# Retention and a SwiGLU feed-forward on one core: an inner level of seven products for three of six gate/value groups in the last two units

## The chip, the cores and the metric

The kernel runs on one core of a Trainium2 chip. The metric is device time in microseconds: the median over several executions. All data are float32. The engines are named as in the profile: PE (TensorE matmuls), PEld (TensorE weight loads), DVE (VectorE), ACT (ScalarE), POOL (GpSimd) and SP (SyncE, whose queue issues nearly all DMAs here).

## The reference

Eight batches of eight heads go through a retention (attention with a decay table instead of a softmax); the result, 4608 tokens of 512 numbers, is normalised and goes through a gated feed-forward network.

```python
scores = scale * np.matmul(q, k.transpose(0, 1, 3, 2))       # q, k, v: (8, 8, 576, 64)
ret = scores * Dmat[None]                                    # gamma ** (i - j) for i >= j, else 0
x = np.matmul(ret, v)                                        # -> (4608, 512)
xn = x / np.sqrt(np.mean(x * x, axis=-1, keepdims=True) + 1e-06) * rms_g
g = xn @ w_gate                                              # (512, 1536)
val = xn @ w_val                                             # (512, 1536)
out = (g / (1.0 + np.exp(-g)) * val) @ w_out                 # (1536, 512)
```

## The kernel before

The tokens are cut into nine units of 512 (`u` = 0 to 8). Units 0 and 1 are computed while weights are still being loaded and rounded, in an order written out by hand (`PLAN`). Units 2 to 8 run in the loop at the end of the kernel: for each unit the six groups of `up`, with the retention of a later unit between the groups as long as there is one (up to u = 6), and then `across`, the output product. The whole is under a manual schedule: each engine, and each DMA queue, works through its instructions in the order in which the program issues them, and waits at the head of its own queue.

**`up(u, n)`, n = 0 to 5.** Even n are gate groups, odd n value groups. A group makes 512 of the 3072 gate and value features as a 2 x 2 block product in the Strassen-Winograd form: seven products of half blocks instead of eight. The seven weight blocks of a group (`A11`, `A12`, `A22`, and the sums `S1` to `S4`) were made once, are kept in DRAM (`w_up_d`) and are loaded anew for each unit. The seven token operands are in `t_of[u]`: four are blocks of `x_of[u]`, three are in `sums_x`; `sums_of_x` makes them at the end of the unit before. Each product is four matmuls (two column halves, two halves of the contraction) of a 128 x 128 weight block with 256 tokens. The order of the products is A11, S2, S1, A12, S3, S4, A22, into four PSUM banks x, y, z, w: A12 accumulates onto x, S4 onto z and A22 onto w, after VectorE has read y, z and w into sums (L651) and ScalarE has copied x (L670). So S4 cannot start before VectorE's addition that reads z is done. A gate group ends in Silu on ScalarE (L665), a value group in a multiplication onto `h` (L663) and in `differences` (L728), which prepares operands of `across`.

**`across(u)`.** Seven products of the same form once more, each cut again into seven 128-column parts with three matmuls each (L814): 147 matmuls. The inner operands are sums over parts of `h`, made by `inner_sums` on GpSimd (L766, L771). They lie in the upper part of the tile `vi` (from column `NV` on), or in `sums_x`. At the end of a unit, `combine` adds the seven parts of four results together: seven GpSimd additions over a stride of four vectors (L1010), issued at the end of `across`, so that they run during the first group of the next unit. `store(u - 1)` then sends the output, from SP, in group 1.

**The ring.** Weights come through `ring`, 17408 columns. The list `pieces` holds every load in the order of use, `places` the columns of each; `used()` marks a piece as done and `refill()` issues, on SP, all loads whose place no longer holds an unused piece (L610). A piece for `up` has 3584 columns, one for `across` 2688; so the loads run about four groups ahead.

**The norm.** In group 5, `square`, `gather` (L473, L467) and `root_1` compute the norm of the next unit: at step i = 4, a matmul on TensorE (L504) that needs the last gathered sum, ahead of the S4 product.

**Tiles.** The retention's tiles (`raw`, `att`) are in two pools of their own that live to the end of the kernel. `x_of` takes turns over three buffers.

Of the kernel before, what the change touches and what calls it, by code (L numbers as in the profile page):

```python
# [10 lines left out]
F32 = mybir.dt.float32  # L11
U32 = mybir.dt.uint32
AF = mybir.ActivationFunctionType
ALU = mybir.AluOpType
P = 128
# [29 lines left out]
def kernel(  # L45
# [11 lines left out]
    nc = tc.nc  # L57
# [3 lines left out]
    NHP = H // 2  # L61
# [4 lines left out]
    U = 512  # L66
    HU = U // 2
    NS = U // P
    NU = NTOK // U
    NH = NF // 2  # L70
    NK = NH // 2
    NG = NH // 2
# [5 lines left out]
    assert S == U + L and NU == B + 1 and NK == 3 and NG == 3  # L78

    const = ctx.enter_context(tc.tile_pool(name="const", bufs=1))  # L80
    raw = ctx.enter_context(tc.tile_pool(name="raw", bufs=1))
    att = ctx.enter_context(tc.tile_pool(name="att", bufs=2))
    xp = ctx.enter_context(tc.tile_pool(name="xp", bufs=3))
    tmp = ctx.enter_context(tc.tile_pool(name="tmp", bufs=4))
    PS = bass.MemoryType.PSUM
    dram = ctx.enter_context(tc.tile_pool(name="dram", bufs=1, space=bass.MemoryType.DRAM))
    banks = ctx.enter_context(tc.tile_pool(name="banks", bufs=8, space=PS))

    def bank(name):
        return banks.tile([P, 512], F32, tag="b", name=name)  # L90
# [4 lines left out]
    def row(name):  # L95
        return tmp.tile([P, U], F32, tag="n", name=name, bufs=3)
# [30 lines left out]
    NV = 4 * 7 * P  # L127
# [371 lines left out]
    def root_1(u):  # L499


        y = t_of[u]
        s = bank(f"ms_{u}")
        nc.tensor.matmul(s, lhsT=ones, rhs=y, start=True, stop=True)  # L504
        e = row(f"e_{u}")
        nc.scalar.activation(
            out=y.bitcast(U32), in_=s.bitcast(U32), func=AF.Relu, bias=guess, scale=-0.5
        )
        nc.scalar.activation(out=e, in_=y, func=AF.Square)
        nc.vector.scalar_tensor_tensor(  # L510
            out=e, in0=e, scalar=-1.0 / DM, in1=s, op0=ALU.mult, op1=ALU.mult
        )
        nc.vector.scalar_tensor_tensor(
            out=y, in0=e, scalar=K0, in1=y, op0=ALU.add, op1=ALU.mult
        )
        nc.scalar.activation(out=e, in_=y, func=AF.Square)
        nc.vector.scalar_tensor_tensor(
            out=e, in0=e, scalar=K1 * K1 / DM, in1=s, op0=ALU.mult, op1=ALU.mult
        )
        t_of[u] = y, e  # L520
# [45 lines left out]

    UP, OUT = 7 * 2 * 2 * P, 7 * NK * P
    w_up_d = dram.tile([2 * NG, P, UP], F32, name="w_up_blocks")  # L570
    w_out_d = dram.tile([7, NK, P, 7 * P], F32, name="w_out_blocks")
    FIRST_ORDER = (A11, S4, A12, S1, S2, S3, A22)
# [7 lines left out]
    pieces = [("out", 0, n) for n in range(7)] + [("out", 1, n) for n in range(4, 7)]  # L580
    N_FIRST = len(pieces)
    for u in range(2, NU):
        pieces += [("up", u, n) for n in range(2 * NG)] + [("out", u, n) for n in range(7)]
    places = []
    at = AT_SUMS
    for kind, u, n in pieces:
        size = UP if kind == "up" else OUT
        if at + size > RING:
            at = AT_SETS if kind == "out" and u < 2 else 0
        places.append((at, at + size))  # L590
        at += size
    n_sent = n_used = 0

    def refill(most=len(pieces)):

        nonlocal n_sent
        while n_sent < min(most, len(pieces)):
            a, z = places[n_sent]
            kind, u, n = pieces[n_sent]
            if any(a < y and x < z for x, y in places[n_used:n_sent]):  # L600
                return
            if u > 1 and n_used < N_FIRST and a < NF * U:
                return
            o = ring[:, a:z]
            if kind == "up":
                src = w_up_d[n]
            else:
                o = o.rearrange("p (c x) -> p c x", c=NK)
                src = w_out_d[order_of(u)[n]].rearrange("c p x -> p c x")
            nc.sync.dma_start(out=o, in_=src)  # L610
            n_sent += 1

    def piece(kind, u, n):
        if kind == "out" and u == 1 and n < 4:
            i = pieces.index(("out", 0, n + 3))
        else:
            i = pieces.index((kind, u, n))
        assert i < n_sent and (i == n_used or kind == "out" and u == 0)
        a, z = places[i]
        if kind == "up":  # L620
            return ring[:, a:z].rearrange("p (b c f) -> p b c f", b=7, c=2)
        return ring[:, a:z].rearrange("p (c n d) -> p n c d", n=7, c=NK)

    def used():
        nonlocal n_used
        n_used += 1
        refill()
# [7 lines left out]
    def up(u, n):  # L635


        m, f = n % 2, n // 2 * 2
        w = piece("up", u, n)

        def product(blk, ps, start):
            for i in range(2):
                for c in range(2):
                    nc.tensor.matmul(  # L644
                        ps[:, i * HU : i * HU + HU], lhsT=w[:, PLACE[blk], c, i * P : i * P + P],
                        rhs=t_of[u][blk][:, c], start=(start and i == c == 0), stop=False,
                        skip_group_check=True,
                    )

        def add(o, a, ps):  # L650
            nc.vector.tensor_tensor(out=o, in0=a, in1=pairs_of(ps), op=ALU.add)  # L651

        def result(f, t, nm, a, ps):

            o = h[:, f : f + 2, t * HU : t * HU + HU]
            c = pairs_of(ps)
            if a is not None:
                c = o
                if m:
                    c = pairs_of(temp(f"{nm}_{u}_{n}")) if nm == "c12" else a  # L660
                add(c, a, ps)
            if m:
                nc.vector.tensor_tensor(out=o, in0=o, in1=c, op=ALU.mult)  # L663
            else:
                nc.scalar.activation(out=o, in_=c, func=AF.Silu)  # L665

        x_, y, z, w_ = (bank(f"{nm}_{u}_{n}") for nm in "xyzw")
        s1, u2, u4 = (pairs_of(temp(f"{nm}_{u}_{n}")) for nm in ("m1", "u2", "u4"))
        product(A11, x_, True)
        nc.scalar.copy(out=s1, in_=pairs_of(x_))  # L670
        yield
        product(S2, y, True)
        add(u2, s1, y)
        yield
        product(S1, z, True)
        add(u4, u2, z)
        yield
        product(A12, x_, False)
        result(f, 0, "c11", None, x_)
        yield  # L680
        product(S3, w_, True)
        result(f + NH, 1, "c22", u4, w_)
        yield
        product(S4, z, False)
        result(f, 1, "c12", u2, z)
        yield
        product(A22, w_, False)
        used()
        result(f + NH, 0, "c21", u2, w_)
        if m:  # L690
            differences(u, f)
        yield

    def up_plain(u, k, n):
# [28 lines left out]
    def differences(u, f):  # L723

        hh = h_1 if u == 1 else h
        b11, b12, b22 = hh[:, f : f + 2, :HU], hh[:, f : f + 2, HU:], hh[:, NH + f : NH + f + 2, HU:]
        for o, a, b in ((t1_of(u)[:, f : f + 2], b12, b11), (b12, b22, b12)):
            nc.vector.tensor_tensor(out=o, in0=a, in1=b, op=ALU.subtract)  # L728
# [548 lines left out]

    with tc.manual_schedule():  # L1280
        start()
        for u in range(2, NU):
            j0 = NHP * (u + 1)
            more = u + 1 < B
            for n in range(2 * NG):
                for i, _ in enumerate(up(u, n)):
                    if n == 1 and i == 4:
                        store(u - 1)
                    if n == 2 * NG - 2 and i == 1:
                        inner_sums(u, 0, 0)  # L1290
                        inner_sums(u, 1, 0)
                    if more and i == 2 and 0 < n <= NHP:
                        if j0 + n < len(jobs):
                            prepare(j0 + n)
                            fetch(j0 + n + 1)
                    if u + 1 < NU and n == 2 * NG - 1:
                        if i < NHP:
                            gather(u + 1, i, square(u + 1, i))
                        elif i == NHP:
                            root_1(u + 1)  # L1300
                    if more and (n, i) == (NHP, 5) and j0 + NHP == len(jobs):
                        values(j0 + NHP - 1)
                if more and n <= NHP and (n or u == 2):
                    if j0 + n < len(jobs):
                        slot(j0 + n, rest=(n > 0))
                    else:
                        carried(j0 + n - 1)
            for i, _ in enumerate(across(u)):
                if u + 1 == NU:
                    continue  # L1310
                if i == 2:
                    root_2(u + 1)
                elif i in (3, 4, 5, 6):
                    scale_x(u + 1, (i - 3,))
                elif i == 8:
                    sums_of_x(u + 1)
# [27 lines left out]
```

## Time and profile before

| | us |
|---|---|
| median of 3 runs | 1106.02 |
| lowest and highest run | 1104.19, 1107.22 |
| profiled execution, span from the first to the last instruction | 1104.5 |
| PE busy | 1091.5 (99%) |
| DVE busy | 751.7 (68%) |
| POOL busy | 458.0 (41%) |
| ACT busy | 339.7 (31%) |
| six groups of `up` in u = 7 | 888.55 to 961.9 |
| `across` in u = 7 | 961.9 to 994.8 |

The profile gives the profiled execution's time as its span, with no time around it; it lies 1.5 us under the median of the runs. HBM reads were 211.92 MB and writes 30.08 MB; the main DMA queue's packets took 69.1% of 16 engines' span. In a line of a timeline the first number is the start, the second the time that the merged instructions took together, then come engine, line, operation, `out<-in` by the program's names, partitions x elements, and the count; what stands in brackets is the idle time of the engine just before, and what ended it. Ends of matmuls are modelled, so the distance between two starts is the safer measure. A float32 matmul appears as two records.

### The profile page before, as it was taken

How to read it: one execution, taken by the hardware profiler on the slowest of the kernel's cores; microseconds unless marked ns; L12 is line 12 of the kernel's file. 1: busy time of each engine (PE TensorE's matmuls, PEld its weight loads, DVE VectorE, ACT ScalarE, POOL GpSimd, SP SyncE). 2: the span in 40 equal slices, each digit the busy share in tenths (PEclk: the TensorE clock that was granted, in tenths of full speed). 3: DMA queues.
4: the chain of work that ended last, by engine and by line, in shares of the span. 5: the costliest groups of instructions: out<-in, count | busy, mean ns of one | idle time of the engine just before them, and what ended most of it. 6: DMA issues, size and time to landing. Idle time of an engine off the chain costs nothing.

```text
span 1104.5 us, 24454 instructions
## 1 busy us (share of the span) xinstructions
PE 1091.5 (99%) x10102; PEld 915.1 (83%) x10102; DVE 751.7 (68%) x1219; ACT 339.7 (31%) x757; POOL 458.0 (41%) x421
## 2 busy tenths in 40 slices
PE   8899999999999999999999999999999999999998
PEld 7654444479988899889988998889888998898898
DVE  3778568877866794678657775668565935594457
ACT  5855564331124412342034303330233111211110
POOL 0026325538430196027802581239321942393236
PEclk9899999999999999999999999999999999999999
DMA  8847777696978866787678865887475755585461
GB/s 211 197 139 259 280 244 217 208 343 185 289 277 227 216 251 226 185 238 235 253 215 199 285 259 149 245 246 284 143 203 198 273 193 176 183 293 158 152 247 43
DMA packets 253871, 243.60 MB, mean 221 GB/s; under 512 B 193216, under 2 KB 213824, under 8 KB 247616
## 3 DMA queue, kind: packets, MB, share of 16 engines
q1 hardware_dynamic: 252320, 241.64, 69.1%
q8 instruction: 79, 1.29, 0.5%
q10 hardware_dynamic: 1440, 0.40, 0.2%
q14 instruction: 32, 0.26, 0.1%
HBM read 211.92 MB, written 30.08 MB: 219 GB/s over the span
## 4 chain that ended last, share of the span: by engine, by line
PE 96%; DVE 1%; issue 1%; ACT 0%; POOL 0%; POOLq 0%; DVEq 0%; ACTq 0%
PE up L704 15%; PE x L644 14%; PE w L644 13%; PE z L644 13%; PE y L644 7%; PE xo L814 6%; PE xp L814 4%; PE zo L814 4%; PE zp L814 3%; PE wo L814 2%; PE yo L814 2%; PE av L379 2%; PE wp L814 2%; PE av L399 2%; PE s L292 2%; PE yp L814 2%
## 5 line engine op out<-in xcount | busy, mean ns | idle before, releaser
L704 PE MATMUL up<-x,ring 128*128 128x512 f32 x384 | 167.1, 595 | 0.0
L644 PE MATMUL x<-x,ring 128*128 128x256 f32 x672 | 161.1, 383 | 0.0
L644 PE MATMUL w<-sums,ring 128*128 128x256 f32 x672 | 158.9, 379 | 0.0
L644 PE MATMUL z<-x,ring 128*128 128x256 f32 x672 | 158.8, 379 | 0.0
L766 POOL TENSOR_TENSOR vi<-h 128x384 f32<-128x384 f32 x32 | 39.5, 1234 | 275.2 <-DVE h L663 266.3
L704 PEld LDWEIGHTS up<-x,ring 128*128 128x128 f32 x384 | 72.3, 190 | 89.3 <-issue 84.8
L644 PEld LDWEIGHTS z<-x,ring 128*128 128x128 f32 x672 | 127.8, 190 | 19.8 <-issue 2.9
L644 PEld LDWEIGHTS w<-sums,ring 128*128 128x128 f32 x672 | 127.7, 190 | 17.2
L644 PEld LDWEIGHTS x<-x,ring 128*128 128x128 f32 x672 | 125.5, 190 | 17.4 <-ACT m L670 0.2
L771 POOL TENSOR_TENSOR vi<-h 128x384 f32<-128x384 f32 (+2 forms) x46 | 46.4, 1009 | 149.5 <-DVE h L663 149.5
L1010 POOL TENSOR_TENSOR vi<-vi 128x512 f32<-128x512 f32 (+1 forms) x77 | 78.1, 1027 | 37.9 <-DVE vi L841 21.5
L644 PE MATMUL y<-sums,ring 128*128 128x256 f32 x336 | 79.4, 379 | 0.0
L670 ACT COPY m<-x 128x512 f32<-128x512 f32 x42 | 24.6, 586 | 173.4 <-PE x L644 173.4
L651 DVE TENSOR_TENSOR h<-u,w 128x512 f32<-128x512 f32 x42 | 28.9, 688 | 67.8 <-PE w L644 67.8
L651 DVE TENSOR_TENSOR u<-m,y 128x512 f32<-128x512 f32 x42 | 28.8, 687 | 63.4 <-PE y L644 62.7
L644 PEld LDWEIGHTS y<-sums,ring 128*128 128x128 f32 x336 | 63.9, 190 | 8.6
L665 ACT ACTIVATE h<-h 128x512 f32<-128x512 f32 x63 | 39.7, 630 | 84.1 <-DVE h L651 84.1
L1130 POOL TENSOR_TENSOR vi<-vi 128x512 f32<-128x512 f32 (+1 forms) x24 | 40.7, 1696 | 30.8 <-DVE vi L1119 17.3
L651 DVE TENSOR_TENSOR u<-u,z 128x512 f32<-128x512 f32 x42 | 28.9, 688 | 33.7 <-PE z L644 33.6
L1130 POOL TENSOR_TENSOR ring<-ring 128x512 f32<-128x512 f32 x24 | 30.4, 1272 | 49.3 <-DMA w_up_blocks<-ring 44.1
L771 POOL TENSOR_TENSOR vi<-vi,h 128x384 f32<-128x384 f32 (+2 forms) x46 | 47.6, 1034 | 3.6
L771 POOL TENSOR_TENSOR vi<-h,vi 128x384 f32<-128x384 f32 (+2 forms) x46 | 46.9, 1019 | 3.6
(314 smaller groups left out, 2086.5 us busy)
## 6 DMA issues: line engine op xcount, KB each, us to landing
ring<-w_out_blocks SPq DMA_DIRECT2D x59, 1344.0 KB, 6.4
ring<-w_up_blocks SPq DMA_DIRECT2D x42, 1792.0 KB, 7.7
w_out_blocks<-vi SPq DMA_DIRECT2D x21, 448.0 KB, 5.9
out_dram<-vi SPq DMA_DIRECT2D x64, 128.0 KB, 3.0
qraw<-in_q_dram SPq DMA_DIRECT2D x96, 72.0 KB, 5.1
kraw<-in_k_dram SPq DMA_DIRECT2D x96, 72.0 KB, 2.5
k<-in_k_dram SPq DMA_DIRECT2D x48, 128.0 KB, 2.9
v<-in_v_dram SPq DMA_DIRECT2D x48, 128.0 KB, 2.8
```

Of the source, the lines that this page charges most:

```text
L292: nc.tensor.matmul(s[e][side(odd), i * L : i * L + L], lhsT=d["kT"][side(e), c * L : c * L + L], rhs=d["qT"][side(e), c * L : c * L + L], ...
L379: mm = nc.tensor.matmul(av[odd][column(j, odd, e), i * L : i * L + L], lhsT=d["v"][side(odd), i, e] if c < NC - 1 else d["vt"][:, e], rhs= ...
L644: nc.tensor.matmul(ps[:, i * HU : i * HU + HU], lhsT=w[:, PLACE[blk], c, i * P : i * P + P], rhs=t_of[u][blk][:, c], start=(start and i == ...
L651: nc.vector.tensor_tensor(out=o, in0=a, in1=pairs_of(ps), op=ALU.add)
L665: nc.scalar.activation(out=o, in_=c, func=AF.Silu)
L670: nc.scalar.copy(out=s1, in_=pairs_of(x_))
L704: nc.tensor.matmul(ps, lhsT=w[:, PLACE[blk], c % 2, i * P : i * P + P], rhs=x_of[u][:, c], start=(c == 0), stop=(c == NHP - 1),)
L766: eng.tensor_tensor(out=i1, in0=x12, in1=x11, op=ALU.subtract)
L771: eng.tensor_tensor(out=o[:, c], in0=a[:, c], in1=b[:, c], op=op)
L814: nc.tensor.matmul(ps, lhsT=lhs[:, c], rhs=w[:, s, c], start=((nm, s // 4) not in first), stop=False, skip_group_check=True,)
L1010: eng.tensor_tensor(out=t[:, :, o], in0=t[:, :, x], in1=t[:, :, y], op=ALU.add)
L1130: nc.gpsimd.tensor_tensor(out=t[o], in0=t[x], in1=t[y], op=op)
```

## The change

In the last two units (`LATE`, u = 7 and 8) groups n = 1, 2 and 3 (`DEEP`) go through a new function, `up_deep`. Each of the seven half-block products is cut once more into seven products of quarters: 49 matmuls of a 128 x 128 weight block with 128 tokens, instead of 28 with 256 tokens. A product takes two PSUM banks (four parts in the first, three in the second), so a group uses all eight. Its parts are read out by VectorE (two additions, of 512 and of 384 elements) or ScalarE (two copies); at the end, GpSimd adds up the seven parts of the four results (`combine_in`, seven additions over four vectors of 128 columns), and the last step, a multiplication on VectorE or Silu on ScalarE (`result`), goes onto a list, `unfinished`, that a later group works off: group 1's multiplications and `differences` in group 2 after its second product, group 2's Silus in group 3 after its fifth, group 3's multiplications and `differences` at (4, 5), (4, 6) and (5, 1), by `FINISH`.

The inner token operands are made by `inner_x`, eight VectorE additions issued in the first step of group 0 of the two units. Its tiles and those of the results take the room of the retention's pools, which are closed then.

The inner weight blocks, 49 for each of the three groups, are made by `inner_blocks` in u = 2, 3 and 4 (one group each): two DMAs copy the three plain blocks of each product from the ring to a DRAM tile, `w_in_d`; GpSimd makes the other four (four subtractions or additions over six blocks, four over one), and `save`, at step 5 of the same group, stores them in two DMAs. The new pieces in the ring have 896 columns, one for each product. The upper part of `vi` is used by `inner_blocks` and by `up_deep`; so the first two `inner_sums` of u = 4, 7 and 8 are issued at (5, 2) instead of (4, 1).

```diff
-    raw = ctx.enter_context(tc.tile_pool(name="raw", bufs=1))
-    att = ctx.enter_context(tc.tile_pool(name="att", bufs=2))
+    retention = ctx.enter_context(ExitStack())
+    raw = retention.enter_context(tc.tile_pool(name="raw", bufs=1))
+    att = retention.enter_context(tc.tile_pool(name="att", bufs=2))
...
+    DEEP = range(1, 4)
+    LATE = (NU - 2, NU - 1)
+    IN_ORDER = (A11, S2, S1, S3, A12, S4, A22)
+    w_in_d = dram.tile([len(DEEP), 7, P, IN], F32, name="w_in_blocks")
...
+            if u in LATE and n in DEEP:
+                pieces += [("in", u, (n, i)) for i in range(7)]
...
+    def inner_blocks(u, n):
+        w = piece("up", u, n)
+        flat = w.rearrange("p b c f -> p b (c f)")
+        d = w_in_d[n - DEEP[0]].rearrange("b p x -> p b x")
+        nc.sync.dma_start(out=d[:, :, :P], in_=flat[:, :, :P])
+        nc.sync.dma_start(out=d[:, :, P : 3 * P], in_=flat[:, :, 2 * P :])
+        t6 = vi[:, NV : NV + 6 * 4 * P].rearrange("p (b s f) -> p b s f", b=6, s=4)
+        t1_ = row(f"inner_{n}").rearrange("p (b s f) -> p b s f", b=1, s=4)
+        groups = (t6, slice(0, 6)), (t1_, slice(6, 7))
+        for t, b in groups:
...
+                nc.gpsimd.tensor_tensor(out=o, in0=x, in1=y, op=op)
+        def save():
+            for t, b in groups:
+                nc.sync.dma_start(out=d[:, b, 3 * P :], in_=t.rearrange("p b s f -> p b (s f)"))
...
+    def inner_x(u):
...
+        x = x_of[u].rearrange("p (a c) (t s h) -> p c s a t h", c=2, t=2, s=2)
+        y = sums_x.rearrange("p i c (s h) -> p c s i h", s=2)
+        for o, v_ in ((deep_x1[0], x), (deep_x2[0], y)):
+            t1_, t3, t2, t4 = (o[:, i] for i in range(4))
+            x11, x12, x21, x22 = v_[:, 0, 0], v_[:, 0, 1], v_[:, 1, 0], v_[:, 1, 1]
+            for r, a, b, op in (
+                (t1_, x12, x11, ALU.subtract), (t3, x22, x12, ALU.subtract),
+                (t2, t3, x11, ALU.add), (t4, x21, t2, ALU.subtract),
+            ):
+                nc.vector.tensor_tensor(out=r, in0=a, in1=b, op=op)
...
+        def product(blk, nm, start):
+            w = piece("in", u, (n, IN_ORDER.index(blk)))
+            if start:
+                held_in[nm] = bank(f"{nm}o_{u}_{n}"), bank(f"{nm}p_{u}_{n}")
+            for i, s in enumerate(PARTS):
+                nc.tensor.matmul(
+                    held_in[nm][i // 4][:, i % 4 * P : i % 4 * P + P], lhsT=w[:, PLACE[s]],
+                    rhs=moving(blk, s), start=(start and i % 4 == 0), stop=False,
+                    skip_group_check=True,
+                )
+            used()
...
+        def combine_in(which):
+            at = PARTS.index
+            for o, x, y in (
+                (A12, A11, A12), (A11, A11, S2), (S1, A11, S1), (S4, S1, S4), (A11, A11, S3),
+                (S3, S1, S3), (A22, A11, A22),
+            ):
+                nc.gpsimd.tensor_tensor(
+                    out=c[:, which, at(o)], in0=c[:, which, at(x)], in1=c[:, which, at(y)],
+                    op=ALU.add,
+                )
...
+        product(A11, "x", True)
+        copy(first, "x")
+        yield
+        product(S2, "y", True)
+        add(first, first, "y")
+        if not m:
+            finish(len(unfinished))
+        yield
+        product(S1, "z", True)
+        add(c[:, C22], first, "z")
+        yield
+        product(S3, "w", True)
+        add(c[:, C22], c[:, C22], "w")
+        yield
+        product(A12, "x", False)
+        copy(c[:, C11], "x")
+        if m:
+            finish(len(unfinished))
...
+        product(S4, "z", False)
+        add(c[:, C12], first, "z")
...
+        product(A22, "w", False)
+        add(c[:, C21], first, "w")
+        if not m:
+            finish()
+        combine_in(slice(2 * split, 4))
+        ends = [lambda i=i: result(i) for i in range(4)]
+        if m:
+            ends[:2] = [lambda: (result(C11), result(C22))]
+            ends[1:] = [lambda: (result(C12), result(C21)), lambda: differences(u, f)]
+        unfinished.extend(ends)
...
+    FINISH = {(z + 1, 5): 1, (z + 1, 6): 1, (z + 2, 1): 1} if z % 2 else {(z + 1, 1): 2, (z + 1, 4): 2}
...
-                for i, _ in enumerate(up(u, n)):
+                deep = u in LATE and n in DEEP
+                save = u == n + 1 and n in DEEP and inner_blocks(u, n)
+                for i, _ in enumerate((up_deep if deep else up)(u, n)):
+                    if save and i == 5:
+                        save()
+                    if u in LATE and (n, i) == (0, 0):
+                        inner_x(u)
...
-                    if n == 2 * NG - 2 and i == 1:
+                    if (n, i) == ((2 * NG - 1, 2) if u in LATE or u == DEEP[-1] + 1 else (2 * NG - 2, 1)):
                         inner_sums(u, 0, 0)
                         inner_sums(u, 1, 0)
...
+                    for _ in range(FINISH.get((n, i), 0) if u in LATE else 0):
+                        unfinished.pop(0)()
```

## The prediction

> **What bounds the kernel now.** I number as the code does: units u = 0 to 8, groups n = 0 to 5, steps i = 0 to 6. The changed units are u = 7 and 8; blocks are made in u = 2, 3 and 4. First the page: engines, chain, a costly group.
>
> ```profile
> span 1104.5 us, 24454 instructions
> ...
> PE 1091.5 (99%) x10102; PEld 915.1 (83%) x10102; DVE 751.7 (68%) x1219; ACT 339.7 (31%) x757; POOL 458.0 (41%) x421
> ...
> PE 96%; DVE 1%; issue 1%; ACT 0%; POOL 0%; POOLq 0%; DVEq 0%; ACTq 0%
> ...
> L644 PE MATMUL y<-sums,ring 128*128 128x256 f32 x336 | 79.4, 379 | 0.0
> ```
>
> TensorE is 96% of the chain, and its products have no idle time before them. An edit gains what it takes from TensorE and costs what makes TensorE wait. The pace is read from its timeline in u = 7, since matmuls overlap and a mean of 379 ns is not a pitch:
>
> ```profile
> 900.64 1.89 PE L644 MATMUL x<-x,ring 128*128 128x256 f32 x8
> 902.37 1.89 PE L644 MATMUL y<-sums,ring 128*128 128x256 f32 x8
> ...
> 912.73 1.89 PE L644 MATMUL x<-x,ring 128*128 128x256 f32 x8
> ...
> 963.27 0.83 PE L814 MATMUL xp<-ring,h 128*128 128x128 f32 x6
> 963.94 0.83 PE L814 MATMUL xo<-ring,vi 128*128 128x128 f32 x6
> ```
>
> A product of `up` (four 256-column matmuls, two records each) takes 1.727 us, a group 12.09. In `across`, three 128-column matmuls take 0.67 us, so one takes 0.2233. Next the timelines of VectorE and GpSimd: `sums_of_x` with GpSimd idle (305) and at work (877), and the start of u = 7.
>
> ```profile
> 305.31 0.68 DVE L563 TENSOR_TENSOR x<-x 128x512 f32<-128x512 f32 x1
> ...
> 877.15 1.48 DVE L563 TENSOR_TENSOR x<-x 128x512 f32<-128x512 f32 x1
> ...
> 889.41 0.55 DVE L841 TENSOR_TENSOR vi<-vi,xp 128x384 f32<-128x384 f32 x1
> 892.28 0.69 DVE L651 TENSOR_TENSOR u<-m,y 128x512 f32<-128x512 f32 x1 [2.32 <-PE y L644]
> 893.93 0.69 DVE L651 TENSOR_TENSOR u<-u,z 128x512 f32<-128x512 f32 x1 [0.97 <-PE z L644]
> ...
> 963.25 0.68 DVE L651 TENSOR_TENSOR c<-u,z 128x512 f32<-128x512 f32 x1
> ```
>
> ```profile
> 878.05 1.44 POOL L771 TENSOR_TENSOR vi<-h 128x384 f32<-128x384 f32 x1
> ...
> 881.95 0.99 POOL L766 TENSOR_TENSOR vi<-t 128x384 f32<-128x384 f32 x1
> ...
> 889.58 9.11 POOL L1010 TENSOR_TENSOR vi<-vi 128x512 f32<-128x512 f32 x7 [2.67 <-DVE vi L841]
> ```
>
> Three things are to be seen. GpSimd's seven additions of `combine` take 9.11 us. VectorE and GpSimd slow each other on operands in SBUF: 0.68 becomes 1.48, 0.99 becomes 1.44; additions from PSUM stay at 0.69. And VectorE works in order: the addition at 963.25 had its product three microseconds earlier and stood behind `root_1`, which waited for ScalarE. Last, stretches of 1 us (columns: stretch; busy PE, PEld, DVE, ACT, POOL; granted clock; DMA share; GB/s) around an early gap in TensorE's work, from 48.11 to 49.43:
>
> ```profile
> 48.00:49.00 1.00, 0.11 (x3) 0.00 (x0) 0.99 (x4) 0.97 (x3) 0.72 (x1) 1.00 0.54 82
> 49.00:50.00 1.00, 0.57 (x5) 0.40 (x4) 0.96 (x2) 1.00 (x4) 0.00 (x0) 0.57 0.55 90
> 50.00:51.00 1.00, 1.00 (x7) 0.71 (x4) 0.85 (x2) 0.73 (x2) 0.00 (x0) 0.50 0.82 134
> 55.00:56.00 1.00, 1.00 (x49) 1.00 (x44) 1.00 (x3) 0.00 (x0) 0.09 (x1) 0.51 0.83 279
> ```
>
> A gap of 1.3 us was followed by 6.6 us at half clock; one of 1.35 us at 11.9 by 3.5 us (15.0 to 18.5).
>
> **The change, part by part.**
>
> *Products.* A deep group has 49 matmuls of 0.2233 us, 10.94 us instead of 12.09 (1.563 per product). Six groups: **−6.9 us**. Operands and columns are those of `across`, so no other pitch is expected.
>
> *VectorE and ScalarE in a deep group.* Each product is read out by additions of 512 and 384 elements (0.69 + 0.55 = 1.24 us), under 1.563: hidden. ScalarE's copies (0.59 + 0.49) and four Silus of 0.63 have its idle time (31% busy).
>
> *Wait A, `inner_x` in group 0.* Eight VectorE additions stand ahead of group 0's first addition, four of 512 and four of 384 elements, all from SBUF. They start when the last addition of `across` ends, 1.4 us after the unit's first product starts (888.55), just as GpSimd begins `combine`. Alone they take 4 × 0.69 + 4 × 0.55 = 5.0 us. The y and z additions would then end at 896.4, before the S4 product is due at 897.2 (888.55 + 5 × 1.727), and nothing stops. In company, at L563's pitch of 1.41 per 512 and 1.05 per 384, they take 9.8 us, and S4, which accumulates onto z, waits until 901.2: 4.0 us. But GpSimd's operation here has 512 elements, 0.27 us longer than L563's partner; alternating pairs of 1.68 and 1.55 for its seven operations make some 11.4 us and a wait of 5.7. I take **5.2 us** per unit, nearer to the contended rows; ends 0 and 6. The Trainium skill (SBUF — State Buffer, "SBUF: two separate sides") calls the shared port pair an exclusive lock, held for a whole instruction. At face value a pair would then take 0.69 + 1.30 us and the wait would be some 8 us, as an estimate from that page; the pairs in the trace overlap more than that (1.41, not 1.69), so the rows decide.
>
> *Wait B, `finish` in group 2.* Group 1 leaves its four combinations to GpSimd: seven additions over four vectors of 128, the shape of the 9.11 us row. They start 0.85 us after group 1's last product (its two read-out additions end then) and end at +10.0. Group 2 puts group 1's four multiplications and two differences on VectorE right after its y addition, at +3.9. VectorE then stands until +10.0, runs six operations of 0.7 (+14.2), and only then adds z (+14.9). Queued behind are z, w and all later read-outs. TensorE reaches S4, which accumulates onto z, at +7.8, and waits **7.2 us** per unit. Ends: 7.0 (combine at 1.27 each) and 9.9 (slowed to 1.68 each). After group 2, the Silus wait on ScalarE until 9.96 us into group 3, with nothing urgent behind them; group 3's multiplications come at the end of group 4, when GpSimd is done: no wait.
>
> *Clock.* Four waits longer than 1.3 us are each followed by half clock for 3.5 to 6.6 us, a loss of half of that, 1.75 to 3.3. I take 2.5 each, **10 us** in all. The Trainium skill (TensorE: Matmul & The Clock Gate, "What's actually happening") has the clock halved only after an idle window of about 3.4 us, in which case A at its low end would be free; the two gaps of 1.3 us show less sufficing here. Waits B are longer than either.
>
> *Group 5 of u = 7.* Two `differences` (0.7 to 1.4 each) move between the gathers on VectorE that feed the norm's matmul L504. That chain has 0.2 us to spare (gather ends 957.4, matmul 957.6): **1.5 us**, ends 0 and 2.8.
>
> *Moved `inner_sums`* (u = 4, 7, 8). GpSimd ran those eight operations at 932.7 to 938.8, then idled until 956.9. They now start about 18 us later, behind the combinations or the save, and end some 6 us before group 5 does. Hidden by that gap; without it `across` would wait up to 6 us.
>
> *Blocks in u = 2 to 4.* GpSimd: 4 operations of 768 elements (1.8 us, from 2.12 for 896) and 4 of 128 (0.45), 9 us after `combine`, in a gap of 38 us. On SP, two copies to DRAM and two saves per unit go between refills and fetches, 3.2 MB; the save stands behind GpSimd, done long before. The ring is about four groups ahead and a 1 MB store lands in 6.3 us: hidden. VectorE is slowed by the shared port in groups with about 1 us of slack per addition: **0.5 us**, ends 0 and 3.
>
> *Transfers.* A deep group takes 458 KB per 1.563 us, 293 GB/s, the same as `across` (1376 KB per 4.69 us), where 284 GB/s moved at a 0.79 DMA share with TensorE never waiting. Nothing is charged. SP issues seven DMAs per deep group where it issued one, each waiting for its place's product, as refills do now.
>
> **Sum**: −6.9 + 2 × 5.2 + 2 × 7.2 + 10 + 1.5 + 0.5 = +29.9 us. The sum stands against the profiled span of 1104.5, giving 1134.4; the median of the runs is 1.5 us above the span, so 1136.
>
> **Rivals.**
> 1. *Only B.* VectorE and GpSimd alternate so that `inner_x` ends before 895.8, and A and its clock loss vanish: −6.9 + 14.4 + 5 + 1.5 + 0.5 = +14.5, 1120. For it: L779, 1536 elements, lost only 0.6 us to company. Against: all four L563 in company took 1.37 or more.
> 2. *Faster.* The order of issue does not hold VectorE at group 1's multiplications, or GpSimd combines in under some 2 us (combination, six operations and z addition must fit before +7.8), and A is hidden: −6.9 + 2 = −5, 1101. Against: 9.11 us in every unit, and 963.25.
> 3. *Transfers bind.* A late unit takes 24.8 MB in about 102 us, 243 GB/s. If queues of smaller DMAs deliver less, say 230, each unit is 5.8 us longer, on top of the sum: 1147. For it: the median of 6.4 us per 1344 KB is 215 GB/s for one transfer alone. Against: 284 GB/s with several under way.
> 4. *The block copies stop units 2 to 4*, SP held behind GpSimd: +3 on top, 1139; inside the range.
>
> **How the numbers follow.** Sum as worked 0.68, only B 0.17, transfers 0.05, faster 0.07, and 0.03 that the two halves cancel within 0.3% (3.3 us, about what a measurement of this kernel can tell from no change). So slower 0.90, same 0.03, faster 0.07. The low end is only B with the lower bounds: −6.9 + 14.0 + 3.5 = +10.6, 1116. With all upper bounds the sum is −6.9 + 12 + 19.8 + 13.2 + 2.8 + 3 = +44; not all will come together, and I cut it at +40, 1146.
>
> **What the profile will show.** Right: in u = 7 and 8 two holes in TensorE's row, some 5 us before S4 of group 0 and some 7 before S4 of group 2, both released by a VectorE addition onto z; VectorE idle some 6 us at group 1's first multiplication, released by GpSimd; `inner_x` operations of 1.4 to 1.7 us; clock at half after each hole; products of 1.56 us otherwise. Wrong: GpSimd's combinations under 4 us, `inner_x` at 0.7 each, or TensorE waiting for a transfer into the ring. The forecast falls most of all if VectorE does not stand at the multiplications.

## The result and the profile after

| | us |
|---|---|
| before, median of 4 runs (1104.19 to 1107.78) | 1106.62 |
| after, median of 4 runs (1143.31 to 1145.86) | 1144.46 |
| ratio, 95% interval | 1.0345 [1.0328, 1.0362] |
| profiled execution after, span | 1142.4 |

The kernel became 37.8 us slower by the medians and 37.9 by the spans (1142.4 − 1104.5). I forecast 1136, by a sum of +29.9, with a range of 1116 to 1146. First the page of the kernel after: span, engines, shares of the chain, and two groups (busy us, mean ns of one, then the idle time before them). Line numbers have moved: L659 is the products' L644 of before, L666 its L651, L1193 its L1010.

```profile
span 1142.4 us, 25234 instructions
...
PE 1096.3 (96%) x10354; PEld 923.1 (81%) x10354; DVE 786.6 (69%) x1265; ACT 347.6 (30%) x775; POOL 541.8 (47%) x487
...
PE 89%; DVE 5%; issue 2%; POOL 2%; SPq 1%; ACT 1%; DMA 0%; POOLq 0%; DVEq 0%; ACTq 0%
...
L659 PE MATMUL z<-x,ring 128*128 128x256 f32 x576 | 140.0, 387 | 11.4 <-DVE u L666 11.4
...
L820 POOL TENSOR_TENSOR deep_c<-deep_c 128x512 f32<-128x512 f32 x42 | 52.8, 1268 | 65.4 <-DVE deep_c L812 40.2
```

TensorE's share of the chain fell from 96% to 89%. VectorE (1 to 5%), GpSimd (0 to 2%) and "issue" (1 to 2%) took the difference. The row of the products onto z, which had no idle time before it, now has 11.4 us, all of it waiting for a VectorE addition. Where these waits are, TensorE's timeline in u = 7 and 8 shows:

```profile
914.66 3.78 PE L659 MATMUL z<-x,ring 128*128 128x256 f32 x8 [5.70 <-DVE u L666]
...
945.54 1.22 PE L792 MATMUL zo<-x,ring 128*128 128x128 f32 x4 [6.52 <-DVE deep_c L812]
...
982.83 1.10 PE L505 MATMUL ms<-sq,ones 128*128 128x512 f32 x2 [0.49 <-DVE sq L468]
...
1034.54 3.67 PE L659 MATMUL z<-x,ring 128*128 128x256 f32 x8 [5.70 <-DVE u L666]
...
1065.22 1.22 PE L792 MATMUL zo<-x,ring 128*128 128x128 f32 x4 [6.52 <-DVE deep_c L812]
```

Two holes per unit: wait A before S4 of group 0 (5.70) and wait B before S4 of group 2 (6.52). The timelines of VectorE and GpSimd show what they stood behind.

```profile
901.48 3.19 DVE L767 TENSOR_TENSOR inner_x<-x 128x512 f32<-128x512 f32 x2
904.70 1.64 DVE L767 TENSOR_TENSOR inner_x<-inner_x,x 128x512 f32<-128x512 f32 x1
...
941.07 2.50 DVE L830 TENSOR_TENSOR h<-h,deep_c 128x512 f32<-128x512 f32 x4 [6.07 <-POOL deep_c L820]
```

```profile
901.18 11.03 POOL L1193 TENSOR_TENSOR vi<-vi 128x512 f32<-128x512 f32 x7 [2.69 <-DVE vi L1024]
...
931.93 9.10 POOL L820 TENSOR_TENSOR deep_c<-deep_c 128x512 f32<-128x512 f32 x7 [19.72 <-issue]
```

`inner_x` takes 1.6 us per operation and `combine` 11.03 in place of 9.11, so each slows the other. Group 1's combination takes 9.10 us, and VectorE idles 6.07 of it at group 1's first multiplication. The clock follows the holes (columns: stretch; busy PE, PEld, DVE, ACT, POOL; granted clock; DMA share; GB/s):

```profile
912.00:916.00 4.00, 1.34 (x3) 1.16 (x4) 3.15 (x5) 0.57 (x1) 0.21 (x1) 0.50 0.00 0
916.00:920.00 4.00, 4.00 (x14) 3.28 (x14) 0.69 (x1) 0.69 (x2) 0.00 (x0) 0.69 0.00 0
...
944.00:948.00 4.00, 2.46 (x11) 2.46 (x12) 3.32 (x7) 0.00 (x0) 0.00 (x0) 0.50 0.00 0
948.00:952.00 4.00, 4.00 (x33) 4.00 (x32) 2.12 (x4) 0.39 (x1) 0.59 (x1) 0.85 0.57 151
```

Taken by unit, from the starts of the first x product of group 0 (before: 306.02, 424.81, 540.92, ..., 888.55, 994.76; after: 304.87, 428.40, 551.90, ..., 900.16, 1020.04), the 37.9 us divide so:

| | before | after | difference |
|---|---|---|---|
| to the start of u = 2 | 306.02 | 304.87 | −1.15 |
| u = 2 | 118.79 | 123.53 | +4.7 |
| u = 3 | 116.11 | 123.50 | +7.4 |
| u = 4 to 6 | 347.63 | 348.26 | +0.6 |
| u = 7 | 106.21 | 119.88 | +13.7 |
| u = 8, to the end | 109.74 | 122.36 | +12.6 |

So the late units lost 26.3 us, near the forecast. (The start of u = 2 lies between 304.8 and 307.3 in the traces of all the runs below, so the 1.15 us is within what it varies by.) Another 12.7 us were lost in u = 2 to 6, where only the blocks are made. TensorE's waits of over 0.6 us between 300 and 700 us, after:

```profile
350.22 0.34 PE L400 MATMUL av<-qT,sum 64*64 64x64 f32 x6 [2.73 <-issue]
...
363.73 1.99 PE L659 MATMUL w<-sums,ring 128*128 128x256 f32 x8 [2.62 <-DVE u L666]
...
481.19 1.99 PE L659 MATMUL w<-sums,ring 128*128 128x256 f32 x8 [1.08 <-DVE u L666]
...
489.26 2.29 PE L659 MATMUL x<-x,ring 128*128 128x256 f32 x5 [2.94 <-issue]
```

Before has one such wait there, 0.86 us at 349.53. The wait at 363.73 can be followed back on ScalarE's and VectorE's timelines, and on SP's queue (in its lines the second number is the time that SP took to issue):

```profile
359.96 0.96 ACT L260 ACTIVATE qraw<-qraw,gp 128x288 f32<-128x288 f32 x2 [6.86 <-DMA qraw<-in_q_dram]
```

```profile
360.95 0.78 DVE L265 STREAM_TRANSPOSE qT<-qraw 128x576 f32<-128x576 f32 x1 [4.30 <-ACT qraw L260]
```

```profile
341.36 0.55 SPq L742 DMA_DIRECT2D w_in_blocks<-vi  x1
342.01 0.52 SPq L742 DMA_DIRECT2D w_in_blocks<-inner  x1
...
345.41 9.80 SPq L163 DMA_DIRECT2D qraw<-in_q_dram  x4
```

The retention's transposes on VectorE stand ahead of the addition that reads w. They waited for ScalarE, and ScalarE 6.86 us for a load of q. That load was issued behind the blocks' two saves and behind two loads into the ring (1792 and 1344 KB); the two ring loads stand ahead of it in before too. The saves land 6.0 and 7.8 us after their issue, by about 350; the two loads into the ring take 11.3 and 14.7 us. All the while the transfer engines are full:

```profile
344.00:348.00 4.00, 3.48 (x140) 2.93 (x139) 2.24 (x7) 1.34 (x3) 0.00 (x0) 1.00 1.09 337
348.00:352.00 4.00, 1.78 (x13) 1.56 (x13) 1.67 (x6) 1.35 (x5) 0.00 (x0) 1.00 0.99 414
352.00:356.00 4.00, 4.00 (x21) 3.51 (x20) 0.72 (x2) 0.85 (x3) 0.00 (x0) 1.00 0.98 368
```

Before has the same stretch without the saves, and in it the engines are nearly full from 340 to 348, and no longer from 348 on:

```profile
340.93 8.15 SPq L162 DMA_DIRECT2D qraw<-in_q_dram  x4
```

```profile
340.00:344.00 4.00, 4.00 (x20) 3.54 (x19) 2.25 (x4) 0.89 (x2) 0.00 (x0) 1.00 0.99 326
344.00:348.00 4.00, 4.00 (x118) 3.44 (x120) 1.60 (x3) 1.67 (x4) 0.00 (x0) 1.00 0.96 392
348.00:352.00 4.00, 3.14 (x59) 2.70 (x50) 2.76 (x10) 1.79 (x7) 0.00 (x0) 1.00 0.80 178
```

There SP began the four issues of q 4.5 us earlier, a load of q took 10.1 us to land (median of the four; 12.5 after), and the transposes began at 355.89, 5.06 us earlier.

### The profile page after: what moved, and what is told of

Its sections match the earlier page's. It is cut to its first block, busy times and chain, and to the rows that moved or that the text cites. A ratio compares the mean times of both kernels' runs of the same rounds, so it can differ in the third digit from the quotient of the medians.

```text
span 1142.4 us, 25234 instructions
## 1 busy us (share of the span) xinstructions
PE 1096.3 (96%) x10354; PEld 923.1 (81%) x10354; DVE 786.6 (69%) x1265; ACT 347.6 (30%) x775; POOL 541.8 (47%) x487
## 4 chain that ended last, share of the span: by engine, by line
PE 89%; DVE 5%; issue 2%; POOL 2%; SPq 1%; ACT 1%; DMA 0%; POOLq 0%; DVEq 0%; ACTq 0%
PE up L887 15%; PE z L659 10%; PE x L659 10%; PE w L659 10%; PE xo L997 6%; PE y L659 5%; PE xp L997 4%; PE zo L997 4%; PE zp L997 3%; PE wo L997 2%; PE yo L997 2%; PE av L380 2%; PE wp L997 2%; PE av L400 2%; PE s L293 2%
## 5 line engine op out<-in xcount | busy, mean ns | idle before, releaser
L659 PE MATMUL z<-x,ring 128*128 128x256 f32 x576 | 140.0, 387 | 11.4 <-DVE u L666 11.4
L659 PE MATMUL x<-x,ring 128*128 128x256 f32 x576 | 139.6, 385 | 2.9 <-issue 2.9
L659 PE MATMUL w<-sums,ring 128*128 128x256 f32 x576 | 136.5, 380 | 3.7 <-DVE u L666 3.7
L659 PEld LDWEIGHTS z<-x,ring 128*128 128x128 f32 x576 | 111.8, 194 | 30.5 <-DVE u L666 12.2
L659 PEld LDWEIGHTS w<-sums,ring 128*128 128x128 f32 x576 | 109.6, 191 | 19.5 <-DVE u L666 4.5
L659 PEld LDWEIGHTS x<-x,ring 128*128 128x128 f32 x576 | 107.5, 191 | 18.2 <-issue 3.1
L1193 POOL TENSOR_TENSOR vi<-vi 128x512 f32<-128x512 f32 (+1 forms) x77 | 81.9, 1077 | 38.0 <-DVE vi L1024 21.5
L820 POOL TENSOR_TENSOR deep_c<-deep_c 128x512 f32<-128x512 f32 x42 | 52.8, 1268 | 65.4 <-DVE deep_c L812 40.2
L659 PE MATMUL y<-sums,ring 128*128 128x256 f32 x288 | 69.9, 386 | 0.5 <-issue 0.5
L666 DVE TENSOR_TENSOR u<-m,y 128x512 f32<-128x512 f32 x36 | 24.7, 686 | 56.1 <-PE y L659 55.5
L659 PEld LDWEIGHTS y<-sums,ring 128*128 128x128 f32 x288 | 55.9, 194 | 8.6 <-issue 0.7
L666 DVE TENSOR_TENSOR h<-u,w 128x512 f32<-128x512 f32 x38 | 26.1, 687 | 52.8 <-PE w L659 52.6
L424 ACT COPY x<-av 128x192 f32<-128x192 f32 (+6 forms) x136 | 37.7, 277 | 31.6 <-PE av L400 30.2
```

What stands on the lines that cost most here:

```text
L424: nc.scalar.copy(out=o, in_=part)
L659: nc.tensor.matmul(ps[:, i * HU : i * HU + HU], lhsT=w[:, PLACE[blk], c, i * P : i * P + P], rhs=t_of[u][blk][:, c], start=(start and i == ...
L820: nc.gpsimd.tensor_tensor(out=c[:, which, at(o)], in0=c[:, which, at(x)], in1=c[:, which, at(y)], op=ALU.add,)
L1193: eng.tensor_tensor(out=t[:, :, o], in0=t[:, :, x], in1=t[:, :, y], op=ALU.add)
```

## The experiments

Each ratio compares with before on the same chip and has its 95% interval; before's medians on these chips lie between 1105.29 and 1106.62. "After" is the 1144.46 us above.

**1. Without wait B.** Group 1's results are no longer worked off behind the second product of group 2. The multiplications fall to the places behind its S4 and A22 products, `differences` to group 3.

```diff
         product(S2, "y", True)
         add(first, first, "y")
-        if not m:
-            finish(len(unfinished))
         yield
```

> Group 1's multiplications and differences are no longer issued after group 2's second product; its two pairs of multiplications follow the additions of products S4 and A22 of group 2, the differences go to group 3. Theory (VectorE stands for GpSimd's combinations at that place, and TensorE's S4 behind it): the 6.5 us wait before S4 of group 2 and the half clock behind it (2.0) go in both late units, 17 us less than the changed kernel, about 1127; the 5.7 us wait in group 0 stays. Rival (the combinations themselves, or the read-outs, are too much for a deep group wherever they are finished): the wait moves to S4 or A22 of group 2 or into group 3 and the time stays within 4 us of 1144.

Measured: 1127.38 us (1126.71 to 1129.87), ratio 1.0191 [1.0174, 1.0208], 17 us less than after. No wait is left in groups 2 and 3; A stays at 5.71 in both units. Wait B and its slow stretch cost 8.5 us per unit; group 2 of u = 7 falls from 19.47 us to 10.94.

**2. Without wait A.** The eight operations of `inner_x` are issued between the products of group 0 rather than ahead of them.

```diff
+    INNER_AT = {0: 2, 1: 1, 2: 1, 4: 1, 5: 2, 6: 1}
...
-                nc.vector.tensor_tensor(out=r, in0=a, in1=b, op=op)
+                inner_ops.append(dict(out=r, in0=a, in1=b, op=op))
...
+                    if u in LATE and n == 0:
+                        for _ in range(INNER_AT.get(i, 0)):
+                            nc.vector.tensor_tensor(**inner_ops.pop(0))
```

> The eight additions of inner_x are issued two, one, one, one, two and one over steps 0, 1, 2, 4, 5 and 6 of group 0, instead of all in step 0. Theory (their place ahead of the y and z additions makes wait A): the 5.7 us wait and the 2.2 us of half clock behind it go in both late units, 15 to 16 us less than the changed kernel, about 1129, with the eight still at 1.5 to 1.7 us each where combine runs beside them. Rival (VectorE has no room for them in group 0 at all): waits of the same sum appear at A22 of group 0 or in group 1's second product, and the time stays above 1140.

Measured: 1129.34 us (1127.23 to 1130.04), ratio 1.0207 [1.0192, 1.0223]. A is gone from both units; B stays, 6.52 and 6.53. The operations beside `combine` still take 1.0 to 1.6 us, but nothing waits for them. A cost 7.6 us per unit: (1144.46 − 1129.34) / 2.

**3. Why A is long: `combine` left out.** The same order as after, but GpSimd idles at the start of u = 7 and 8.

```diff
-        if u and not last:
+        if u and u + 1 not in LATE and not last:
             combine(slice(0, 4), nc.gpsimd)
```

> Leaves out the seven GpSimd additions of combine at the end of units 6 and 7, so that the output rows of these units are not combined; all else as in the changed kernel. Theory (the shared SBUF access makes the eight additions slow): they take 0.69 and 0.55 us, some 5 us together, S4 of group 0 does not wait, and the time is 15 to 16 us less than the changed kernel, about 1129. Rival (VectorE's own work at the start of the unit is late enough without GpSimd): the additions shrink but S4 still waits 2 us or more, and the time is above 1135.

Measured: 1128.17 us, ratio 1.0206 [1.0185, 1.0226]. On VectorE's timeline:

```profile
899.86 1.29 DVE L767 TENSOR_TENSOR inner_x<-x 128x512 f32<-128x512 f32 x2
901.18 0.69 DVE L767 TENSOR_TENSOR inner_x<-inner_x,x 128x512 f32<-128x512 f32 x1
```

With GpSimd idle the operations take 0.69 and 0.56 us, the eight 4.9 us in all (899.86 to 904.7), and S4 does not wait. So the order alone does no harm, nor does the company alone (experiment 2): A needs both.

**4. The blocks' DMAs left out.** The twelve transfers into `w_in_d` are not issued; GpSimd still makes the blocks, and the late units load columns of `w_up_d` of the same size.

```diff
-        nc.sync.dma_start(out=d[:, :, :P], in_=flat[:, :, :P])
-        nc.sync.dma_start(out=d[:, :, P : 3 * P], in_=flat[:, :, 2 * P :])
...
-            for t, b in groups:
-                nc.sync.dma_start(out=d[:, b, 3 * P :], in_=t.rearrange("p b s f -> p b (s f)"))
```

> Leaves out the twelve DMAs that copy and save the inner blocks in units 2 to 4 (the late units load other columns of the plain blocks of the same size, so their products are not the reference's); GpSimd still makes the blocks. Theory (these transfers stand ahead of the loads of q, k and v, and of instructions, in units 2 and 3): units 2 to 4 take 116 us each as before, 11 us less than the changed kernel, about 1133. Rival (GpSimd's block arithmetic slows VectorE there): the time stays within 3 us of 1144.

Measured: 1132.57 us (1129.59 to 1134.01), ratio 1.0236 [1.0217, 1.0255], 11.9 us less than after. Units 2 to 4 take 118.98, 116.09 and 116.11 us, as before.

**5. GpSimd's work for the blocks left out, their DMAs kept.** Four of the eight operations per group, those over six blocks, are not issued.

```diff
-        for t, b in groups:
+        for t, b in groups[1:]:
             a11, a21, a12, a22 = (flat[:, b, i * P : i * P + P] for i in range(4))
```

> Leaves out GpSimd's four large block additions in units 2 to 4 (six of the seven inner blocks of each product keep stale sums, so the late products are not the reference's); the twelve DMAs stay, with the same bytes. Theory (the transfers cost the 11 us of units 2 to 4): the time stays within 3 us of the changed kernel, 1144. Rival (the arithmetic has a share through the shared SBUF access): some 3 to 8 us less.

Measured: 1147.34 us (1144.54 to 1150.51), ratio 1.0382 [1.0351, 1.0414]; no gain. Units 2 to 4 take 122.98, 123.23 and 117.10 us, after 123.53, 123.50 and 116.78. With experiment 4 this shows that the transfers cost the 12 us, and that GpSimd's four large operations per group, and what they take from VectorE, have no measurable part in it.

**6. The same DMAs from another queue.** Does SP's order hold the loads up, or the transfer engines that all queues share?

```diff
-        nc.sync.dma_start(out=d[:, :, :P], in_=flat[:, :, :P])
+        nc.scalar.dma_start(out=d[:, :, :P], in_=flat[:, :, :P])
```

(The other three likewise.)

> The twelve block DMAs are issued at the same places from ScalarE's queue instead of SP's. Theory one (order in SP's queue: the loads of q, k and v wait behind these transfers): they now run beside them, the late transposes go, and most of the 11 us does, about 1135. Theory two (the same 16 DMA engines are full, whichever queue issues): the loads and the instruction fetches are as late as before, about 1143.

Measured: 1148.79 us (1147.93 to 1151.41), ratio 1.039 [1.0367, 1.0413]; above both expectations and not better than after. The waits "issue" of over 0.4 us are gone between 300 and 700 us, and the waits for the addition ahead of A22 have grown, on TensorE's timeline:

```profile
363.43 3.55 PE L659 MATMUL w<-sums,ring 128*128 128x256 f32 x8 [5.09 <-DVE u L666]
...
486.13 3.64 PE L659 MATMUL w<-sums,ring 128*128 128x256 f32 x8 [4.79 <-DVE u L666]
...
621.29 2.53 PE L659 MATMUL w<-sums,ring 128*128 128x256 f32 x8 [2.56 <-DVE h L666]
```

The waits moved from "issue" to VectorE, and u = 4 now has one too. The other queue brought no gain, but the edit does not tell the two theories apart, since it moved the transfers in time as well. ScalarE's queue issues the saves of u = 2 as soon as GpSimd is done, 15 us earlier than SP did (341.36), and SP's loads of k beside them take three times as long to issue as in after (329.63, 2.32 us):

```profile
325.95 0.40 ACTq L742 DMA_DIRECT2D w_in_blocks<-vi  x1
```

```profile
328.53 7.36 SPq L163 DMA_DIRECT2D kraw<-in_k_dram  x4
```

All that SP issues behind them comes later, and the next loads of q start at 346.29, no earlier than in after (345.41). Whether the loads of q in the kernel after were held by their order behind the blocks in SP's queue, or by the transfer engines that all queues share, stays open. What TensorE's sequencer waits for in an "issue" gap no view names; that it was an instruction fetch is a guess that no run tests.

**7. The blocks earlier in the unit.** The two copies and GpSimd's work start at step 2 of group 0, the saves at step 3 of group 1, while group 1 brings the first loads of q, k and v.

```diff
-                save = u == n + 1 and n in DEEP and inner_blocks(u, n)
...
-                    if save and i == 5:
+                    if u - 1 in DEEP and (n, i) == (0, 2):
+                        save = inner_blocks(u, u - 1)
+                    if u - 1 in DEEP and (n, i) == (1, 3):
                         save()
```

> The blocks are copied and made from group 0's third step on, where SP has no loads of q, k and v, and saved after group 1's fourth step, behind that group's loads; amount and queue stay. Theory (place, not amount): the waits of units 2 and 3 go and the time is some 9 to 11 us less than the changed kernel, about 1134. Rival (amount: 3.2 MB more per unit is too much for the DMA engines wherever it is put): the time stays above 1140.

Measured: 1136.6 us (1134.7 to 1138.48), ratio 1.0276 [1.0252, 1.0299], 7.9 us less than after: short of the 9 to 11 expected. u = 3 and 4 fall to 117.0 and 116.2 us; u = 2 keeps a wait of 2.96 us at 362.04. By this, two thirds of the 12 us were the place.

**8. All three repairs.** Experiments 1, 2 and 7 in one kernel.

> The later finish, the spread inner_x and the early blocks together; the computation is the reference's. If the three losses are all there is, what remains of the changed kernel is its gain of 1.14 us in each of six deep groups, less some 0.5 to 1 us in group 5 of unit 7: 1106 - 6 = 1100, a ratio of 0.994 to the kernel before. If there is a fourth loss that the others covered (transfers into the ring, VectorE in group 2), it shows now: a ratio of 1.00 or more.

Measured: 1103.84 us, median of 12 runs (1099.99 to 1106.23), against 1106.14 (17 runs); ratio 0.9979 [0.9966, 0.9992]. The late units now take 103.55 and 106.25 us (to the end at 1101.2), 2.7 and 3.5 less than before, where the products alone promised 3.45 each. In u = 2 and 3 there are still 2.8 and 1.4 us to be paid for the blocks, about what is missing to the 1100 expected; no wait of the late units exceeds the 0.48 us before the norm's matmul, so no fourth loss shows in them.

**9. The blocks one unit later.** As experiment 8, with u = 3 to 5 in place of 2 to 4.

```diff
-                    if u - 1 in DEEP and (n, i) == (0, 2):
-                        save = inner_blocks(u, u - 1)
-                    if u - 1 in DEEP and (n, i) == (1, 3):
+                    if u - 2 in DEEP and (n, i) == (0, 2):
+                        save = inner_blocks(u, u - 2)
+                    if u - 2 in DEEP and (n, i) == (1, 3):
                         save()
```

> All three edits as in the run with all three, with the blocks made one unit later each: u = 3, 4 and 5 in place of 2, 3 and 4, still from step 2 of group 0. In that run u = 2 was still some 2.8 us longer than before and u = 3 some 1.5, u = 4 nothing. Theory one, u = 2 is the tight unit (it follows the hand-ordered start and its own q and k loads are the latest): u = 2 falls back to 118.8 us, u = 3 pays what it paid, and the time is 1101 to 1102. Theory two, it is the block itself, the first one of the sequence or group 1's piece: the loss moves with it to u = 3, and the time stays at 1104.

Measured: 1102.13 us, median of 8 runs (1098.04 to 1104.55), against 1105.29 (13 runs); ratio 0.9971 [0.9957, 0.9985]. This is the best version found, faster than both kernels. u = 2 is back at 118.85 us; u = 3 takes 117.48, u = 4 116.09 and u = 5 117.52. The loss of u = 2 did not move along, so u = 2 was the tight unit. Against experiment 8 the medians differ by less than the intervals tell apart; the unit lengths carry this reading.

**10. The same bytes in small pieces.** As experiment 9, with one pair of copies per step and one save at every second step.

```diff
-        nc.sync.dma_start(out=d[:, :, :P], in_=flat[:, :, :P])
-        nc.sync.dma_start(out=d[:, :, P : 3 * P], in_=flat[:, :, 2 * P :])
+        def plain(b):
+            nc.sync.dma_start(out=d[:, b, :P], in_=flat[:, b, :P])
+            nc.sync.dma_start(out=d[:, b, P : 3 * P], in_=flat[:, b, 2 * P :])
...
+                    at = 7 * n + i
+                    if u - 2 in DEEP and 2 <= at < 9:
+                        plain(at - 2)
+                    if u - 2 in DEEP and 12 <= at < 26 and at % 2 == 0:
+                        save((at - 12) // 2)
```

> As the shifted run, with the same 3.2 MB per unit cut into one pair of copies per step for the plain blocks (steps (0,2) to (1,1)) and one save of a block at every second step from (1,5) on, in place of four large transfers. Theory one, what the block costs is the burst, in which the transfer engines are full for 7 to 8 us and everything else waits behind it: with the same bytes spread over some 38 us the waits of TensorE in u = 3 to 5 fall under 1 us in all, and the time is 1100 to 1101. Theory two, the bytes cost wherever they go, or the 21 issues on the queue do: the time is that of the shifted run or more.

Measured: 1112.23 us (1110.96 to 1113.04), ratio 1.0063 [1.0051, 1.0075], 10 us more than experiment 9. Theory one did not hold: the same bytes in small pieces cost more. SP's queue and TensorE in u = 5:

```profile
715.05 1.05 SPq L748 DMA_DIRECT2D w_in_blocks<-vi  x2
716.19 11.35 SPq L163 DMA_DIRECT2D qraw<-in_q_dram  x4
```

```profile
733.75 2.88 PE L659 MATMUL w<-sums,ring 128*128 128x256 f32 x8 [4.40 <-DVE h L666]
```

The spread saves reach into groups 2 to 4, among the loads of q and k, whose issues take 11.35 us here (8.35 in experiment 9, at 708.63). ScalarE then waits 8.52 us for q, and TensorE 4.40. u = 3, 4 and 5 are 2.4, 3.8 and 6.5 us longer than before. So spreading them among such loads is worse than experiment 9's large transfers, the copies ahead of the unit's first such loads and the saves right behind them. How much of the 10 us comes from the place and how much from the number of transfers was not separated.

## Why the prediction was right, and its step that was not

The direction, the two mechanisms in the late units and the range held; the sum was 8 us short. One step, the blocks, was 12.2 us short, and the other terms, with the earlier start of u = 2, took back 4.2.

- **Products**: predicted 10.94 us per deep group; group 1 of u = 7 takes 920.10 to 931.04, 10.94. The forecast's −6.9 stands.
- **Wait A**: predicted 5.2 (0 to 6), measured 5.70. Of the two ways of pairing I gave, the longer, with pairs of 1.68 and a wait of 5.7, was the right one. Here the Trainium skill (SBUF — State Buffer, "SBUF: two separate sides") is borne out in kind only: an exclusive lock would have made an estimated 8 us, and the measured pairs of 1.64 for operations that take 0.69 and 1.30 alone overlap in part. Experiments 2 and 3 show that the order and the company are both needed.
- **Wait B**: predicted 7.2 (7.0 to 9.9), measured 6.52. The measured value lies under my lower end. My own figures (0.85 + 9.11 + 6 × 0.7 + 0.69 − 7.82) give 7.0, not 7.2; most of the rest is that VectorE's six operations after GpSimd took 3.8 us in place of 4.2: they end at 944.89, 13.85 after 931.04, where I had +14.2.
- **Clock**: predicted 2.5 per hole, 10 in all. Group 0 of u = 7 lost 7.85 us, of which 5.70 are the hole, and group 2 lost 8.53 with a hole of 6.52; in u = 8 they lost 7.65 and 8.43. That leaves 1.9 to 2.15 beyond each hole, 8.0 in all. The price is no constant: in the traces of experiments 1 to 3, holes of the same lengths cost 2.7 to 3.3 us beyond the hole. Nor is every gap of over 1.3 us followed by half clock, as the two early gaps had let me think. In after the wait of 2.94 us that ends at 489.26 was, those of 2.73 and 2.62 us, ending at 350.22 and 363.73, were not. The stretches behind the first and the last of these:

```profile
490.00:494.00 4.00, 4.00 (x11) 3.12 (x10) 0.00 (x0) 0.58 (x1) 1.39 (x4) 0.50 0.86 103
```

```profile
364.00:368.00 4.00, 4.00 (x149) 3.45 (x148) 3.93 (x6) 1.44 (x5) 3.84 (x6) 1.00 0.90 329
```

- **Group 5 of u = 7**: predicted 1.5 (0 to 2.8); it lost 0.73, of which 0.49 are idle.
- **Transfers in the late units**: nothing was charged, and TensorE waits for no load into the ring there. The rival is refuted. The moved `inner_sums` cost nothing either, as forecast: `across` in u = 7 takes 32.82 us, 32.83 before.
- **Blocks in u = 2 to 4: the step that failed.** I took 0.5 us, with ends of 0 and 3, since "the ring is about four groups ahead and a 1 MB store lands in 6.3 us: hidden". Units 2 to 6 lost 12.7 us by their lengths, and 11.9 went with the DMAs in experiment 4. What I named as cover, the ring's lead, covers the ring's own loads. The loads of q, k and v have a lead of one group only. They share SP's queue and the transfer engines with 3.2 MB of blocks per unit, which I set beside the ring alone. Which of the two held them was not separated (experiment 6). The 0.5 us that I did charge, for VectorE beside GpSimd, has no measurable part (experiment 5). Rival 4 named the place, but its reason (SP held behind GpSimd) is not in the trace, and its 3 us were a quarter of the loss.

The terms of the late units came to 29.4 us in the forecast and 26.3 in the trace; the blocks came to 0.5 and 12.7, and the start of u = 2 lies 1.15 us earlier. 26.3 + 12.7 − 1.15 gives the 37.9. That the time lies in the range, 1.5 us under its upper end, is partly luck: that end, made of the upper bounds of all the other terms, left room for a loss that was not in the sum.

## What to carry to other kernels

An addition that is "hidden by a slack" on an engine that works in order also delays everything queued behind it: find the next product that needs an accumulator, and count to there. Before charging a bulk transfer at nothing, list every load that shares its queue or the transfer engines with it and take the one with the shortest lead, not the one with the most bytes. Nearly all the loss here came from where work was put: with the same 49 products and three changes of place, the kernel was 0.2 to 0.3% faster than before in place of 3.4% slower.

## What the runs showed of the hardware

- Holes of 5.70 to 6.54 us in TensorE's work were each followed by a stretch at half clock. In after it cost 1.9 to 2.15 us, and 2.7 to 3.3 in the traces of experiments 1 to 3. In after, group 0's holes of 5.70 us cost no less than group 2's of 6.52.
- Shorter gaps were followed by half clock only sometimes: one of 2.94 us (489.26) was, at a granted clock of 0.50, those of 2.73 and 2.62 us (350.22, 363.73) were not, at 1.00.
- Moving twelve transfers from SP's queue to ScalarE's gave no gain (1148.79 against 1144.46). There the saves of u = 2 were issued 15 us earlier, and the issues of the k loads beside them took 7.36 us in place of 2.32.
- With the transfers on SP's queue TensorE has gaps released by nothing that the profile shows (2.73 and 2.94 us, "issue"). In the run without the DMAs the only one of over 0.4 us was 1.09 us, in before 0.86, and with the same DMAs on ScalarE's queue there was none.
- The same 3.2 MB per unit cost 1.4 us in u = 3 and in u = 5 and nothing in u = 4 as four large transfers in groups 0 and 1 (experiment 9), and 2.4, 3.8 and 6.5 us in u = 3, 4 and 5 as 21 small ones that reached into groups 2 to 4 (experiment 10).
